# GpSimd's share of the k products in three instructions, with VectorE's share ordered ahead of them

## The chip, the cores and the metric

The kernel runs on one core of a Trainium2 chip. The metric is the time of one execution in microseconds (us) on the device, as a median of several runs. A profile of one execution gives the durations of the single instructions. Some runs are slow (over 1.5% above the fastest of the same kernel). Ratios and means below are of fast runs, unless slow ones are named; medians are of all runs.

## The reference

A linear attention with polynomial features feeds a feed-forward layer:

```python
# q, k, v: (4 batches, 4 heads, 1088, 32); S1, S2: (8, 32)
def phi(x):                       # 64 features: all products of 8 by 8 projections
    a = einsum('rd,bhsd->bhsr', S1, x); b = einsum('rd,bhsd->bhsr', S2, x)
    return einsum('bhsi,bhsj->bhsij', a, b).reshape(*x.shape[:-1], 64)
q_p, k_p = phi(q), phi(k)
kv = einsum('bhsf,bhsd->bhfd', k_p, v);  z = k_p.sum(axis=2)
attn = einsum('bhsf,bhfd->bhsd', q_p, kv) / (einsum('bhsf,bhf->bhs', q_p, z)[..., None] + 1e-6)
h = maximum(x @ w_in, 0)          # x: attn as 4352 tokens of 128; w_in: 128 x 2048
out = (h * h) @ w_out
```

## The kernel before

TensorE's time is filled by the feed-forward part: per step one matmul with w_in into PSUM (tile pg, L908), a Relu from PSUM to SBUF (gt, on ScalarE L918 or VectorE L920), a square (g, L902 or L929), and a matmul with w_out (po, L939). While one chunk of tokens goes through it, the attention of later chunks is slipped in between by a planner, which places each small task into a step of the loop. The tasks in question are the features of k of batch n = 1, 2, 3: TensorE makes the projections (qk from kq, L431), VectorE turns them (fs, L352), and the 64 products per token and head are made half on VectorE and half on GpSimd (kp, L361):

```python
    def a_kp2(b, g):                               # L357
        fs = st[b, "fs"]
        ...
        (nc.vector if g == 0 else nc.gpsimd).tensor_tensor(
            out=_ap(st[b, "kp2"], 0, 128, 128 * NT * g, [[64, 2 * NT], [8, 8], [1, 8]]),
            in0=_ap(fs, 0, 128, 2 * g, [[32, 2 * NT], [4, 8], [0, 8]]),
            in1=_ap(fs, 0, 128, 2 * g + 1, [[32, 2 * NT], [0, 8], [4, 8]]),
            op=mult,
        )
    ...
    def k_tasks(n):                                # L1288
        for g in range(2):
            P.add(("fs", n, g), "DVE", 0.45, [("kf", n)], a_fs, n, g, slow=n > 1 and 1.2)
        P.at["X"] = max(P.at["X"], P.at["fs", n, 1])
        P.add(("kp", n, 1), "POOL", 3.15, [("fs", n, 1)], a_kp2, n, 1)
        if n == 1:
            x_tasks(0, 2)
        P.add(("kp", n, 0), "DVE", 1.36, [("fs", n, 0)], a_kp2, n, 0, slow=n > 1 and 1.5)
```

`_ap(tile, partition, partitions, offset, [[step, count], ...])` is a free access pattern in fp32 elements. In batch 1 the chain de, rd, rb, x, ax (`x_tasks`) runs on VectorE and ScalarE between the two products. In batches 2 and 3 VectorE has another turn (qT, L325) just ahead of its product and a Relu of the feed-forward part (L920) just behind it.

Of the kernel before, what the change touches and what calls it, by code (L numbers as in the profile page):

```python
# [15 lines left out]
def _ap(t: bass.AP, p0: int, np_: int, off: int, free):  # L16

    p = list(t.ap)[0]
    return bass.AP(
        t.tensor, t.offset + p0 * p[0] + off, [[p[0], np_]] + [list(d) for d in free]  # L20
    )
# [52 lines left out]
def kernel(  # L74
# [22 lines left out]
    NT = (S + 127) // 128  # L97
# [141 lines left out]
    st = {}  # L239
# [114 lines left out]
                _ap(kf, 0, 128, 0, [[16, 2 * NT], [2, 8], [1, 2]]),  # L354
            )

    def a_kp2(b, g):  # L357
        fs = st[b, "fs"]
        if (b, "kp2") not in st:
            st[b, "kp2"] = wpool.tile([128, 2 * 128 * NT], F32, tag="kp2", name="kp2")  # L360
        (nc.vector if g == 0 else nc.gpsimd).tensor_tensor(  # L361
            out=_ap(st[b, "kp2"], 0, 128, 128 * NT * g, [[64, 2 * NT], [8, 8], [1, 8]]),
            in0=_ap(fs, 0, 128, 2 * g, [[32, 2 * NT], [4, 8], [0, 8]]),
            in1=_ap(fs, 0, 128, 2 * g + 1, [[32, 2 * NT], [0, 8], [4, 8]]),
            op=mult,
        )

# [737 lines left out]
    for lo, n in ((0, 2), (2, 3)):  # L1105
        nc.vector.tensor_tensor(
            out=_ap(kp4, 0, 128, 256 * lo, [[64, 4 * n], [8, 8], [1, 8]]),
            in0=_ap(fs4, 0, 128, 64 * lo, [[16, 4 * n], [2, 8], [0, 8]]),
            in1=_ap(fs4, 0, 128, 64 * lo + 1, [[16, 4 * n], [0, 8], [2, 8]]),
# [53 lines left out]
    P = _Plan(NS + 4, {"PE": 0.95, "DVE": 1.2, "ACT": 0.6, "POOL": 5.0, "SP": 9.0})  # L1163
    for m in range(B * 3 - 1):
        b, ch = divmod(m, 3)
# [98 lines left out]
    def x_tasks(b, ch):  # L1264
        if b == 0:
            P.add(("dT", b, ch), "DVE", 0.58, [("nd", b, ch)], a_dT, b, ch)
            P.add(("rd", b, ch), "DVE", 0.4, [("dT", b, ch)], a_rd, b, ch, lag=0)
            P.add(("rb", b, ch), "DVE", 0.58, [("rd", b, ch)], a_rb, b, ch, lag=0)
            P.add(("x", b, ch), "DVE", 0.56, [("rb", b, ch)], a_x, b, ch, lag=0)
        else:  # L1270
            P.at["x", b, ch] = P.at["nd", b, ch]
        P.add(("ax", b, ch), "ACT", 0.5, [("x", b, ch)], a_ax, b, ch)
        P.add(("sum", b, ch), "PE", 0.17, [("ax", b, ch)], a_sum, b, ch)
        P.add(("rs", b, ch), "DVE", 0.53, [("sum", b, ch)], a_rs, b, ch)
        if b > 0:
            P.add(("xs", b, ch), "DVE", 0.56, [("rs", b, ch)], a_xs, b, ch, lag=0)
        P.add(("s2", b, ch), "DVE", 0.53, [("sum", b, ch)], a_s2, b, ch)
        if b == 0:
            P.add(("xs", b, ch), "POOL", 0.95, [("rs", b, ch)], a_xs, b, ch)
            P.at["N"] = P.at["s2", b, ch]  # L1280
        else:
            P.at["N"] = max(P.at["s2", b, ch], P.at["xs", b, ch])
        P.add(("bt", b, ch), "POOL", 1.0, [("s2", b, ch)], a_beta, b, ch)
        if (b, ch) == (B - 1, 2):
            P.add(("bcol", b, ch), "DVE", 0.5, [("bt", b, ch)], a_bcol, b, ch, lag=3)
        ready(b, ch)

    def k_tasks(n):  # L1288
        for g in range(2):
            P.add(("fs", n, g), "DVE", 0.45, [("kf", n)], a_fs, n, g, slow=n > 1 and 1.2)  # L1290
        P.at["X"] = max(P.at["X"], P.at["fs", n, 1])
        P.add(("kp", n, 1), "POOL", 3.15, [("fs", n, 1)], a_kp2, n, 1)
        if n == 1:
            x_tasks(0, 2)
        P.add(("kp", n, 0), "DVE", 1.36, [("fs", n, 0)], a_kp2, n, 0, slow=n > 1 and 1.5)

    def turn_q(n, i):
        c0, c1 = 384 * i, min(384 * i + 384, S)
# [34 lines left out]
    P.add(("set", 1), "DVE", 0.6, [], a_set, 1, first=8)  # L1333
    nd_tasks(0, 2)
    k_tasks(1)
    kv_tasks(1)
    turn_q(1, 0)
# [4 lines left out]
    for m in range(3, 3 * B):  # L1342
        n, ch = divmod(m, 3)
        if m == 99:
            P.cap["DVE"] = CAP
        if ch == 0 and n + 1 < B:
            turn_k(n + 1)
        nd_tasks(n, ch)
        if True:
            x_tasks(n, ch)  # L1350
        if m + 1 < 3 * B:
            feature_tasks(*divmod(m + 1, 3))
        if False:
            x_tasks(n, ch)
        if ch == 0 and n + 1 < B:
            k_tasks(n + 1)
        if ch == 1 and n + 1 < B:
            kv_tasks(n + 1)
        if m + 2 < 3 * B:
            turn_q(*divmod(m + 2, 3))  # L1360
# [88 lines left out]
```

## Time and profile before

| | before |
|---|---|
| time, median of 3 runs (lowest, highest) | 200.17 us (199.97, 200.66) |
| span of the profiled run | 199.2 us |
| TensorE busy | 186.3 us, 94% |
| ScalarE, VectorE, GpSimd busy | 66%, 62%, 43% |
| product of 1152 elements on VectorE | 2.21, 4.34, 4.36 us |
| product of 1152 elements on GpSimd | 2.70 us, three times |

TensorE is full but for a few places, so the question at each place is which wait ends last in front of TensorE. The prediction shows the lines. Four instructions of TensorE serve below as marks along the run. They are from the timeline (start us, duration us, engine, line, operation); the first three are the k projections of batches 1, 2 and 3, the fourth is a projection of q behind batch 3's products:

```profile
29.70 0.69 PE L431 MATMUL qk<-kq,sk 64*32 64x288 f32 x16
...
57.01 0.72 PE L431 MATMUL qk<-kq,sk 64*32 64x288 f32 x16
...
101.17 0.71 PE L431 MATMUL qk<-kq,sk 64*32 64x288 f32 x16
...
116.54 0.56 PE L564 MATMUL qk<-qT,sw 64*64 64x160 f32 x8
```

In windows of 0.1 us the granted clock of this run is 0.50 from 113.3 to 116.7 us, behind batch 3's products, and 1.00 on both sides; these 3.4 us are called the half-speed window or the clock drop below.

The stretch from one mark to the next holds the products of one batch: 57.01 - 29.70 = 27.31 us for batch 1, 44.16 for batch 2, 15.37 for batch 3. Before the first mark lie 29.7 us of start, behind the last 82.7 us of tail.

### The profile page before, as it was taken

To read this page: it belongs to the slowest core of one execution; us is meant where nothing else is said; L and a number is where in the kernel's file an instruction comes from. 1 tells how busy PE (TensorE), PEld (TensorE's weight loads), DVE (VectorE), ACT (ScalarE), POOL (GpSimd) and SP (SyncE) were. 2 spreads that over 40 slices of the span, in tenths; PEclk is the share of its full clock that TensorE was granted. 3 is DMA by queue.
4 is the path that set the end of the run, shared out by engine and by line. 5 is a ranking of instruction groups with operands and counts; after the bars stand their busy time and mean duration, and the time that the engine had idled before them with its cause. 6 is when DMAs were issued, how large, how long until landed. Compare 5 with 4: busy or idle time off the path is not lost.

```text
span 199.2 us, 4283 instructions
## 1 busy us (share of the span) xinstructions
PE 186.3 (94%) x1468; PEld 108.4 (54%) x1468; DVE 123.5 (62%) x284; ACT 130.6 (66%) x322; POOL 85.0 (43%) x166
## 2 busy tenths in 40 slices
PE   7997999899999699999999599999999999999990
PEld 2663655365655346555656346555465655555980
DVE  3958868965649856374459745486291754637750
ACT  3335795767949566877759348569495766856840
POOL 5825545473329161534549123333646441351000
PEclk9999999999999999999999879999999999999999
DMA  5699243020256121422155120121022030200201
GB/s 171 173 303 276 71 106 142 0 43 0 53 112 181 40 33 35 129 41 51 27 121 160 33 31 19 34 41 38 21 42 60 0 63 21 33 10 0 43 0 33
DMA packets 30079, 13.91 MB, mean 70 GB/s; under 512 B 20202, under 2 KB 28778, under 8 KB 30058
## 3 DMA queue, kind: packets, MB, share of 16 engines
q1 hardware_dynamic: 29910, 13.58, 27.7%
q8 instruction: 11, 0.18, 0.4%
q14 instruction: 10, 0.08, 0.2%
q10 hardware_dynamic: 148, 0.07, 0.1%
HBM read 8.80 MB, written 2.23 MB: 55 GB/s over the span
## 4 chain that ended last, share of the span: by engine, by line
PE 77%; DVE 9%; issue 4%; DMA 3%; ACT 2%; SPq 2%; POOL 1%; ACTq 0%; DVEq 0%
PE po L939 48%; PE pg L908 13%; PE kvp L393 3%; PE ndn L637 2%; PE qk L564 2%; PE pt L956 2%; SPq L141 2%; PE nd L778 2%; DMA kn<-in_k_dram 1%; PE rep L1084 1%; DVE de L668 1%; ACT gt L918 1%; DMA ft<-ft 1%; DMA vn<-in_v_dram 1%; DVE fs L352 1%
## 5 line engine op out<-in xcount | busy, mean ns | idle before, releaser
L939 PE MATMUL po<-g,w_o 128*128 128x384 f32 (+3 forms) x386 | 145.1, 462 | 0.1
L918 ACT ACTIVATE gt<-pg 128x384 f32<-128x384 f32 (+2 forms) x139 | 65.2, 472 | 37.2 <-PE pg L908 36.5
L939 PEld LDWEIGHTS po<-g,w_o 128*128 128x128 f32 x386 | 65.9, 191 | 37.9 <-issue 20.1
L902 ACT ACTIVATE g<-gt 128x384 f32<-128x384 f32 (+1 forms) x146 | 72.2, 506 | 10.4 <-DVE gt L920 10.0
L908 PE MATMUL pg<-xT,w_in 128*128 128x384 f16 (+2 forms) x193 | 61.1, 318 | 4.7 <-DVE gt L920 4.1
L929 POOL TENSOR_TENSOR g<-gt 128x384 f32<-128x384 f32 (+1 forms) x44 | 34.4, 789 | 57.9 <-ACT gt L918 57.8
L920 DVE TENSOR_SCALAR gt<-pg 128x384 f32<-128x384 f32 (+1 forms) x54 | 28.8, 535 | 27.9 <-PE pg L908 20.3
L908 PEld LDWEIGHTS <-w_in 128*128 128x128 f16 x193 | 19.2, 99 | 22.9 <-issue 5.1
L599 POOL TENSOR_TENSOR qp<-tq,bs 128x384 f32<-128x384 f32 (+1 forms) x18 | 14.2, 810 | 16.9 <-DVE bs L591 16.9
L573 DVE STREAM_TRANSPOSE tq<-qk 128x384 f32<-128x384 f32 (+1 forms) x9 | 5.0, 561 | 13.7 <-PE qk L564 8.7
L738 POOL TENSOR_TENSOR bt<-s 128x384 f32<-128x384 f32 (+1 forms) x10 | 8.2, 816 | 7.2 <-DVE s L712 7.2
L361 DVE TENSOR_TENSOR kp<-fs 128x1152 f32<-128x1152 f32 x3 | 10.9, 3636 | 0.0
L985 DVE SCALAR_TENSOR_TENSOR sc<-po,bt 128x384 f32<-128x384 f32 (+1 forms) x9 | 4.8, 528 | 6.4 <-PE po L939 6.3
L361 POOL TENSOR_TENSOR kp<-fs 128x1152 f32<-128x1152 f32 x3 | 8.1, 2704 | 1.3 <-DVE fs L352 1.3
L971 POOL COPY br<-beta 32x3 f32<-32x3 f32 x32 | 5.8, 182 | 6.0 <-DVE beta L861 4.8
L720 DVE TENSOR_SCALAR rs<-ndn 128x384 uint32<-128x384 uint32 (+1 forms) x9 | 4.8, 536 | 3.7 <-PE ndn L704 3.5
L393 PEld LDWEIGHTS kvp<-kp,vn 128*32 128x32 f32 x288 | 5.4, 109 | 2.7 <-PE pg L908 1.6
L393 PE MATMUL kvp<-kp,vn 128*32 128x64 f32 x288 | 6.5, 223 | 0.0
L1060 PE MATMUL warm<-zero 128*128 128x512 f16 x16 | 5.2, 483 | 1.2 <-DVE zero L169 1.2
L325 DVE STREAM_TRANSPOSE qT<-qn 128x384 f32<-128x384 f32 (+1 forms) x12 | 6.3, 526 | 0.0
L956 PE MATMUL pt<-w_o,g 128*128 128x128 f32 x32 | 5.7, 274 | 0.0
L637 PE MATMUL ndn<-ft,kw 64*32 64x192 f32 (+1 forms) x144 | 5.6, 347 | 0.0
(147 smaller groups left out, 156.3 us busy)
## 6 DMA issues: line engine op xcount, KB each, us to landing
vn<-in_v_dram SPq DMA_DIRECT2D x32, 64.0 KB, 2.0
kn<-in_k_dram SPq DMA_DIRECT2D x3, 544.0 KB, 4.8
qn<-in_q_dram SPq DMA_DIRECT2D x3, 544.0 KB, 4.1
ft<-u SPq DMA_DIRECT2D x24, 48.0 KB, 1.9
out_dram<-oT SPq DMA_DIRECT2D x24, 48.0 KB, 1.9
w_in<-in_moe_w_in_dram SPq DMA_DIRECT2D x2, 512.0 KB, 8.4
w_o<-in_moe_w_out_dram SPq DMA_DIRECT2D x2, 512.0 KB, 9.9
ft<-ft SPq DMA_DIRECT2D x12, 48.0 KB, 1.8
```

What stands on the lines that cost most here:

```text
L361: (nc.vector if g == 0 else nc.gpsimd).tensor_tensor(out=_ap(st[b, "kp2"], 0, 128, 128 * NT * g, [[64, 2 * NT], [8, 8], [1, 8]]), in0=_ap( ...
L393: nc.tensor.matmul(st[b, "kvp"][32 * h : 32 * h + 32, 0:64], _ap(vn[b], 0, n, v0 + dv * h, [[1, 32]]), kp[0:n, at[h] : at[h] + 64], start= ...
L599: nc.gpsimd.tensor_tensor(out=_ap(qp, 0, 128, 0, [[32, m], [8, 4], [1, 8]]), in0=_ap(st[b, "tq", ch], 0, 128, 4 * e, [[32, m], [1, 4], [0, ...
L637: nc.tensor.matmul(nd[32 * h : 32 * h + 32, 512 * g : 512 * g + n], st[b, "kw"][64 * g : 64 * g + 64, 32 * h : 32 * h + 32], st[b, ch, "ft ...
L738: nc.gpsimd.tensor_tensor(out=bt[:, 0:n], in0=st[b, "s2", ch][:, 0:n], in1=st[b, "s2", ch][:, 0:n], op=mult)
L902: nc.scalar.activation(dst, src, Square)
L908: nc.tensor.matmul(pg[:, c0:c1], w_in[:, 128 * c : 128 * c + 128], st[b, "xT"][:, 384 * ch + c0 : 384 * ch + c1],)
L918: nc.scalar.activation(gt[:, c0:c1], pg[:, c0:c1], Relu)
L920: nc.vector.tensor_scalar(out=gt[:, c0:c1], in0=pg[:, c0:c1], scalar1=0.0, scalar2=None, op0=amax)
L929: (nc.vector if on[1] == "DVE" else nc.gpsimd).tensor_tensor(out=g2[:, c0:c1], in0=gt[:, c0:c1], in1=gt[:, c0:c1], op=mult)
L939: nc.tensor.matmul(st["po", b, ch][:, c0:c1], w_o[:, 128 * c : 128 * c + 128], g2s[i][1][:, c0:c1], start=first, stop=(c == NFF - 1), skip ...
L956: nc.tensor.matmul(st["pt"][:, 0:128], g2s[i][1][:, 0:128], w_o[:, 128 * c : 128 * c + 128], start=(c == 0), stop=(c == NFF - 1),)
```

## The change

The intent is that the two products of a batch no longer hold each other up: VectorE's comes first, right behind the turns, and GpSimd's follows in three pieces, so that a VectorE instruction that waits for GpSimd can start behind a piece and need not wait for the whole product. In the profile before, one did come in between two GpSimd instructions: xT ends at 39.52, VectorE's ob (from 38.77) at 39.92, and bt, which takes 1.04 us, at 40.50.

```diff
-    def a_kp2(b, g):
+    def a_kp2(b, g, lo=0, hi=NT):
         ...
-            out=_ap(st[b, "kp2"], 0, 128, 128 * NT * g, [[64, 2 * NT], [8, 8], [1, 8]]),
-            in0=_ap(fs, 0, 128, 2 * g, [[32, 2 * NT], [4, 8], [0, 8]]),
-            in1=_ap(fs, 0, 128, 2 * g + 1, [[32, 2 * NT], [0, 8], [4, 8]]),
+            out=_ap(st[b, "kp2"], 0, 128, 128 * (NT * g + lo), [[64, 2 * (hi - lo)], [8, 8], [1, 8]]),
+            in0=_ap(fs, 0, 128, 64 * lo + 2 * g, [[32, 2 * (hi - lo)], [4, 8], [0, 8]]),
+            in1=_ap(fs, 0, 128, 64 * lo + 2 * g + 1, [[32, 2 * (hi - lo)], [0, 8], [4, 8]]),
 ...
-        P.add(("kp", n, 1), "POOL", 3.15, [("fs", n, 1)], a_kp2, n, 1)
+        if n > 1:
+            P.add(("kp", n, 0), "DVE", 1.36, [("fs", n, 1)], a_kp2, n, 0, lag=0)
+        for i in range(3):
+            P.add(("kp", n, 1), "POOL", 0.95, [("kp", n, 0) if n > 1 else ("fs", n, 1)],
+                  a_kp2, n, 1, 3 * i, 3 * i + 3)
         if n == 1:
             x_tasks(0, 2)
-        P.add(("kp", n, 0), "DVE", 1.36, [("fs", n, 0)], a_kp2, n, 0, slow=n > 1 and 1.5)
+            P.add(("kp", n, 0), "DVE", 1.36, [("fs", n, 1)], a_kp2, n, 0)
```

## The prediction

> **What bounds the kernel now.** I read the page's busy table first: TensorE works 186.3 of 199.2 us, so an engine that is not TensorE matters only where it makes TensorE wait. The table of 40 slices (5 us each) tells where TensorE is not full: apart from start and end, the digits fall to 6 in slice 14 (64.7 to 69.7 us) and to 5 in slice 23 (109.6 to 114.5).
>
> ```profile
> PE 186.3 (94%) x1468; PEld 108.4 (54%) x1468; DVE 123.5 (62%) x284; ACT 130.6 (66%) x322; POOL 85.0 (43%) x166
> ...
> PE   7997999899999699999999599999999999999990
> ```
>
> Then the groups of line L361, the products of the k features, which the change touches. Each batch n = 1, 2, 3 has one such instruction on VectorE and one on GpSimd, of the same 1152 elements.
>
> ```profile
> L361 POOL TENSOR_TENSOR kp<-fs x3: 2699/2701/2711, 31.4 to 106.8; 128x1152 f32<-128x1152 f32 x3
> L361 DVE TENSOR_TENSOR kp<-fs x3: 2210/4342/4356, 35.4 to 107.2; 128x1152 f32<-128x1152 f32 x3
> ```
>
> The durations are minimum, median, maximum. GpSimd always takes 2.70 us; VectorE takes 2.21 us once and 4.34 and 4.36 us twice. The timeline tells why. These lines are batch 2 (start us, duration, engine, line):
>
> ```profile
> 62.60 2.70 POOL L361 TENSOR_TENSOR kp<-fs 128x1152 f32<-128x1152 f32 x1
> 62.61 0.47 DVE L325 STREAM_TRANSPOSE qT<-qn 128x320 f32<-128x320 f32 x1
> ...
> 63.00 4.34 DVE L361 TENSOR_TENSOR kp<-fs 128x1152 f32<-128x1152 f32 x1
> ...
> 67.27 0.54 DVE L920 TENSOR_SCALAR gt<-pg 128x384 f32<-128x384 f32 x1
> ...
> 67.86 0.32 PE L908 MATMUL pg<-xT,w_in 128*128 128x384 f16 x1 [1.81 <-DVE gt L920]
> ```
>
> GpSimd's product ends at 65.30, VectorE's at 67.34, which is 2.04 later and close to the 2.21 us of the undisturbed one: VectorE's instruction waited for the whole of GpSimd's. Behind it stands a Relu of the feed-forward part (gt, L920), and TensorE cannot refill that PSUM bank before: it idles until 67.86. The steps before are 0.81 us apart (L908 at 65.09), so 65.90 was due: 1.96 us lost. Batch 3 is the same at 106.76 to 112.04: L908 at 108.81, due at 109.62, came at 112.04, 2.42 us lost. Batch 1 differs, and there VectorE's product is not the victim:
>
> ```profile
> 31.43 2.70 POOL L361 TENSOR_TENSOR kp<-fs 128x1152 f32<-128x1152 f32 x1 [1.31 <-DVE fs L352]
> ...
> 31.78 2.38 DVE L668 TENSOR_SCALAR de<-dT 128x10 f32<-128x10 f32 x1
> ...
> 35.51 0.56 ACT L693 ACTIVATE ax<-x,tiny 128x320 bf16<-128x320 f32 x1 [1.43 <-DVE x L684]
> ```
>
> An addition on ten elements takes 2.38 us, ending at 34.16, right after GpSimd's 34.13. The chain de, rd, rb, x, ax hangs on it, and TensorE's small sum and the Relus and squares queued behind ax on ScalarE. TensorE's last matmul before is over at 35.34; with a sum between, the next L939 was due at about 35.66 and came at 36.91: 1.25 us lost. The three losses are 5.6 us.
>
> One cost comes behind the third. The windows view (last three numbers: clock, DMA share, GB/s) shows a slower TensorE clock only there:
>
> ```profile
> 108.00:112.00 4.00, 1.78 (x8) 0.88 (x6) 4.00 (x3) 1.69 (x4) 1.48 (x1) 1.00 0.27 66
> 112.00:116.00 4.00, 3.96 (x17) 1.83 (x24) 1.92 (x4) 1.84 (x4) 0.83 (x1) 0.66 0.24 35
> 116.00:120.00 4.00, 4.00 (x37) 2.15 (x22) 1.80 (x6) 2.53 (x6) 1.73 (x3) 0.91 0.06 10
> ```
>
> By 116.61, when the 16 ndn matmuls are done, it has cost some 1.2 us against batch 2's same steps (L908 to the end of ndn takes 3.07 us there, 67.86 to 70.93, and 4.57 here, 112.04 to 116.61; part of that is a wait for a Relu).
>
> [...] batch 2's transposes (ft, 61.66) and L728 (one PSUM, one SBUF input, 60.72) run at 0.57 and 0.56 us beside GpSimd products. [...] fs is read with a step of four fp32 elements here, at 2210/1152 = 1.9 ns per element, against 0.95/768 = 1.2 ns for batch 0's product (L1106), which reads with a step of two. So VectorE's own cost is 2.2 us, not the 1.36 that the source plans with. [...] A clock of 0.66 and 0.91 in the two stretches is what one half-speed window of 3.4 us makes (0.34 x 4 + 0.09 x 4 = 1.7 us of clock lost).
>
> **The change, part by part.** The order of the built instructions, compared engine by engine, shows less than the diff suggests. TensorE, ScalarE and SyncE are the same. On GpSimd the three products become three each of 384 elements, in the same place. On VectorE only batches 2 and 3 change: the product and the transpose qT swap places; in batch 1 the order stays. No wait is added between the two engines' products, so GpSimd does not wait for VectorE by a semaphore.
>
> (a) GpSimd pieces. 2.70/3 = 0.90 us each, near the 0.83 us of its other 384-element products; total unchanged. [...] GpSimd xT (to 39.52) and bt follow each other at once, VectorE's two-input ob (38.77) ends at 39.92, and bt takes 1.04 us where the 320-element products of L929 and L599 take 0.72 and 0.74 on average: ob came between.
>
> (b) Batch 1. de gets in after piece 1, at 31.43 + 0.90 = 32.33 instead of 34.13, 1.8 earlier. rd, rb, x take until 33.66 (35.48 before). ScalarE is free for ax at 34.08, ends at 34.6; then Relu to 35.0, square to 35.5, in time for the L939 due at 35.66. Gain 1.25 us. VectorE's product then waits for piece 3 (34.1) and ends at 36.2 instead of 37.61.
>
> (c) Batches 2 and 3. VectorE's product is ready at 62.61, where qT started; GpSimd's first piece at 62.60. It is nearly a tie, the same 10 ns in batch 3 (106.76 and 106.77). *GpSimd first:* VectorE runs from 63.5 to 65.6, qT adds 0.39, the Relu runs 65.95 to 66.5, L908 at 66.55: 1.3 gained of 1.96. Batch 3 likewise: product to 109.7, Relu 110.05 to 110.6, L908 at 110.65: 1.4 of 2.42. *VectorE first:* product to 64.8, Relu from 65.15, no stall in batch 2; in batch 3 L908 at 109.88, 2.15 gained. But batch 2 then meets the moves of ft by DMA: the last of the four is issued at 66.6 to 67.1 and needs 1.9 us to land, so at 69.05; TensorE's ndn, at 70.38 before, would be due at 68.42. Of 1.96 some 0.6 is lost, 1.35 stays.
>
> Sum: GpSimd first 1.25 + 1.3 + 1.4 = 3.95; VectorE first 1.25 + 1.35 + 2.15 = 4.75. The clock drop should vanish in both, since batch 3's pause shrinks from 2.25 us to 1 or less. But the run with this profile took 201.02 us and the timed ones 200.17, so I suppose that most timed runs do not have it, and count 0.2.
>
> GpSimd's later work does not suffer: its pieces end near 67.5 and 111.7; the next square comes at 69.72 and 113.83, each about 2 us earlier after the change, and k v (L393) is 10 us away.
>
> **The rivals.** *The pieces follow so closely that VectorE never gets between.* Then de still waits to 34.1, and in batches 2 and 3 the product with qT behind it ends 0.4 later: 200.2 to 201. Against it stands ob between xT and bt. *Something else takes the place of the wait.* TensorE runs earlier against DMA (the ft moves, above) and against ScalarE, which in 63 to 65 us is full (its squares release L939 with waits of 0.2 to 0.3 us per step); half the gain could go: 197.5 to 198. For it: ScalarE's 4.00 of 4.00 us busy in 60 to 64 us. Against it: it catches up as soon as Relus fall to VectorE, and I found its squares in time in (b) and (c). *The clock drop is in most of the timed runs:* then 1 us more is gained, 195.
>
> **Range and chances.** Tie weighted evenly: (3.95 + 4.75)/2 = 4.35, plus 0.2, less 0.35 because small waits usually return: 4.2 us, so 196.0. Low 194.7 is VectorE first with most of the clock gain; high 197.8 is half the gain. The 2% line is at 196.17, just beside the estimate, so faster gets only 0.54; slower would need the first rival and more.
>
> **What would show it.** Right: de under 1 us; VectorE's product in batches 2 and 3 at 3.1 us (GpSimd first) or 2.2 (VectorE first, GpSimd's first piece then near 3 us); the Relu behind it near 66 or 65; TensorE's slices 14 and 23 at 8 or 9; clock 1.00 throughout. Wrong: VectorE's product still at 4.3 us or more; or short, but TensorE waiting at ndn or on ScalarE squares for what was saved.

## The result, and the profile after

The changed kernel takes 194.74 us (median of 4 runs, 194.59 to 195.64) beside 200.41 us of the kernel before (4 runs, 199.97 to 201.84). The ratio is 0.971, with a 95% interval of 0.966 to 0.977, which is a gain of 4.6 to 6.9 us. Ratios here are the mean time of one kernel's fast runs over that of the other's of the same rounds, so they are not quite the ratio of the medians quoted. By the means (200.66 and 194.93) the gain is 5.7 us. I had predicted 4.2 us; the result is at or beyond the low end of my range, according to which of the two figures for before one starts from. So the direction was right and the size too small.

First the page's busy rows of the changed kernel, engines and the 40 slices, with the granted clock in tenths:

```profile
PE 184.9 (96%) x1468; PEld 108.2 (56%) x1468; DVE 118.6 (61%) x284; ACT 130.6 (68%) x322; POOL 91.0 (47%) x172
...
PE   7997999999999999999999999999999999999990
...
PEclk9999999999999999999999999999999999999999
```

The 6 and the 5 in TensorE's row are gone. VectorE is busy 4.9 us less, GpSimd 6.0 us more: the wait has moved from one engine to the other, and is counted as busy time on both. The groups of L361 (minimum, median, maximum in ns) show the same:

```profile
L361 POOL TENSOR_TENSOR kp<-fs x9: 1015/1032/3140, 31.5 to 107.8; 128x384 f32<-128x384 f32 x9
L361 DVE TENSOR_TENSOR kp<-fs x3: 2218/2232/2832, 33.7 to 103.7; 128x1152 f32<-128x1152 f32 x3
```

VectorE's product takes 2.2 us in batches 2 and 3; GpSimd's first piece takes up to 3.14 us there, which is its wait. The timeline of batch 2:

```profile
61.39 5.11 POOL L361 TENSOR_TENSOR kp<-fs 128x384 f32<-128x384 f32 x3
...
61.39 2.23 DVE L361 TENSOR_TENSOR kp<-fs 128x1152 f32<-128x1152 f32 x1
...
63.97 0.52 DVE L920 TENSOR_SCALAR gt<-pg 128x384 f32<-128x384 f32 x1
...
64.68 0.33 PE L908 MATMUL pg<-xT,w_in 128*128 128x384 f16 x1
```

Both products start in the same hundredth of a microsecond, VectorE's takes 2.23 us (2.21 where nothing held it up in the kernel before) while GpSimd's three pieces stretch to 5.11 us, and the Relu behind it comes at 63.97, in time: L908 carries no wait. Batch 1:

```profile
31.45 2.98 POOL L361 TENSOR_TENSOR kp<-fs 128x384 f32<-128x384 f32 x3 [1.31 <-DVE fs L352]
...
31.81 0.69 DVE L668 TENSOR_SCALAR de<-dT 128x10 f32<-128x10 f32 x1
...
34.01 0.55 ACT L693 ACTIVATE ax<-x,tiny 128x320 bf16<-128x320 f32 x1
```

The small addition de gets in behind the first piece and takes 0.69 us instead of 2.38; ax comes 1.5 us earlier. The windows around batch 3 (the last three figures of a line are the mean clock, the DMA share and GB/s) show no clock below 1.00:

```profile
104.00:108.00 4.00, 3.88 (x17) 2.22 (x16) 3.91 (x6) 3.61 (x9) 4.00 (x3) 1.00 0.45 136
108.00:112.00 4.00, 4.00 (x37) 1.85 (x36) 2.26 (x7) 2.16 (x5) 2.24 (x3) 1.00 0.30 45
```

And the four marks:

```profile
29.73 0.69 PE L431 MATMUL qk<-kq,sk 64*32 64x288 f32 x16
...
55.79 0.72 PE L431 MATMUL qk<-kq,sk 64*32 64x288 f32 x16
...
98.14 0.71 PE L431 MATMUL qk<-kq,sk 64*32 64x288 f32 x16
...
109.87 0.50 PE L564 MATMUL qk<-qT,sw 64*64 64x160 f32 x8
```

The stretches are 26.06, 42.35 and 11.73 us. So batch 1 gave 1.25 us, batch 2 1.81, batch 3 3.64; the tail grew by 0.3 us (82.7 to 83.0). Of batch 3's 3.64, the pause itself is 2.14: L908 lost 2.42 us before, and now it starts at 106.88 where 105.79 + 0.81 = 106.60 was due, 0.28 lost:

```profile
105.79 0.33 PE L908 MATMUL pg<-xT,w_in 128*128 128x384 f16 x1
...
106.88 0.32 PE L908 MATMUL pg<-xT,w_in 128*128 128x384 f16 x1
```

The other 1.50 us go with the half-speed clock behind the pause (0.50 from 113.3 to 116.7 us before, 1.00 in both windows here), a short wait for a Relu in it included; the run batch3_old below has the pause without the drop, and there this part is 15.37 - 13.84 = 1.53 us.

### The profile page after: what moved, and what is told of

It reads as the page before. It is cut to its first block, busy times and chain, and to the rows that moved or that the text cites.

```text
span 192.9 us, 4289 instructions
## 1 busy us (share of the span) xinstructions
PE 184.9 (96%) x1468; PEld 108.2 (56%) x1468; DVE 118.6 (61%) x284; ACT 130.6 (68%) x322; POOL 91.0 (47%) x172
## 3 DMA queue, kind: packets, MB, share of 16 engines
HBM read 8.80 MB, written 2.23 MB: 57 GB/s over the span
## 4 chain that ended last, share of the span: by engine, by line
PE 86%; DVE 4%; SPq 3%; DMA 2%; ACT 1%; issue 1%; POOL 1%; ACTq 0%
PE po L939 53%; PE pg L908 15%; PE kvp L393 3%; PE ndn L637 2%; PE warm L1060 2%; PE qk L564 2%; PE pt L956 2%; SPq L141 2%; PE nd L778 2%; PE rep L1084 1%; SPq L626 1%; DMA ft<-u 1%; ACT gt L918 1%; DVE kp L361 1%; DMA vn<-in_v_dram 1%
## 5 line engine op out<-in xcount | busy, mean ns | idle before, releaser
L939 PE MATMUL po<-g,w_o 128*128 128x384 f32 (+3 forms) x386 | 144.1, 459 | 0.0
L918 ACT ACTIVATE gt<-pg 128x384 f32<-128x384 f32 (+2 forms) x139 | 65.4, 473 | 36.3 <-PE pg L908 35.6
L939 PEld LDWEIGHTS po<-g,w_o 128*128 128x128 f32 x386 | 65.6, 190 | 33.3 <-ACT g L902 16.9
L908 PE MATMUL pg<-xT,w_in 128*128 128x384 f16 (+2 forms) x193 | 60.9, 317 | 0.7 <-ACT xT L880 0.3
L929 POOL TENSOR_TENSOR g<-gt 128x384 f32<-128x384 f32 (+1 forms) x44 | 34.9, 801 | 46.3 <-ACT gt L918 46.2
L908 PEld LDWEIGHTS <-w_in 128*128 128x128 f16 x193 | 19.1, 99 | 21.9 <-issue 4.1
L361 POOL TENSOR_TENSOR kp<-fs 128x384 f32<-128x384 f32 x9 | 13.2, 1498 | 1.3 <-DVE fs L352 1.3
L361 DVE TENSOR_TENSOR kp<-fs 128x1152 f32<-128x1152 f32 x3 | 7.3, 2427 | 0.0
```

What stands on the lines that cost most here:

```text
L361: (nc.vector if g == 0 else nc.gpsimd).tensor_tensor(out=_ap(st[b, "kp2"], 0, 128, 128 * (NT * g + lo), [[64, 2 * (hi - lo)], [8, 8], [1, ...
L908: nc.tensor.matmul(pg[:, c0:c1], w_in[:, 128 * c : 128 * c + 128], st[b, "xT"][:, 384 * ch + c0 : 384 * ch + c1],)
L918: nc.scalar.activation(gt[:, c0:c1], pg[:, c0:c1], Relu)
L929: (nc.vector if on[1] == "DVE" else nc.gpsimd).tensor_tensor(out=g2[:, c0:c1], in0=gt[:, c0:c1], in1=gt[:, c0:c1], op=mult)
L939: nc.tensor.matmul(st["po", b, ch][:, c0:c1], w_o[:, 128 * c : 128 * c + 128], g2s[i][1][:, c0:c1], start=first, stop=(c == NFF - 1), skip ...
```

## The experiments

The table gives the same stretches for each profiled run, from the same four marks, so that it can be read beside each experiment. The time up to the first mark is not touched by any edit, and yet it differs by up to 2.5 us between profiled runs; this is probably a large part of the noise in the timed medians (the timed runs have no profile to show it). The first four experiments ran on one chip, the last four on another, each beside its own runs of the kernel before (medians 202.13 and 200.64 us, means of the fast ones 201.58 and 200.77). So expected times, which start from 200.2 us, are to be compared by gains and ratios.

| kernel | to mark 1 | batch 1 | batch 2 | batch 3 | tail |
|---|---|---|---|---|---|
| before | 29.70 | 27.31 | 44.16 | 15.37 | 82.7 |
| changed | 29.73 | 26.06 | 42.35 | 11.73 | 83.0 |
| split_only | 32.15 | 26.06 | 42.59 | 12.26 | 82.4 |
| order_only | 31.45 | 27.31 | 42.44 | 11.73 | 83.0 |
| tie | 30.35 | 26.07 | 42.99 | 12.63 | 82.9 |
| de_reduce | 30.31 | 25.78 | 44.16 | 15.56 | 82.6 |
| after_again | 30.52 | 26.07 | 42.56 | 11.75 | 82.1 |
| batch3_old | 30.34 | 26.06 | 42.41 | 13.84 | 82.8 |
| layout | 30.57 | 25.86 | 42.40 | 11.45 | 82.7 |
| pieces63 | 30.33 | 26.48 | 42.55 | 11.73 | 82.3 |

**split_only: the pieces alone.** To the kernel before, with `a_kp2` taking lo and hi as in the change:

```diff
-        P.add(("kp", n, 1), "POOL", 3.15, [("fs", n, 1)], a_kp2, n, 1)
+        def three():
+            for i in range(3):
+                a_kp2(n, 1, 3 * i, 3 * i + 3)
+        P.add(("kp", n, 1), "POOL", 3.15, [("fs", n, 1)], three)
```

> The kernel before with GpSimd's products in three pieces and VectorE's order left as it was (qT ahead of the product). Theory [...]: batch 1 as in the changed kernel, de near 0.7 us and 1.2 us gained; in batches 2 and 3 GpSimd is first by 0.4 us, VectorE's product takes about 2.7 us instead of 4.34, the Relu behind it comes some 1.65 us earlier, 1.6 us gained in each. Sum 4.4 us, and 0.6 for the clock drop in the mean of the timed runs: about 195.5 us. Rival (the new order in VectorE does the work, the pieces add little): 199 us or more, VectorE's product still at 4 us.

Measured: correct; 196.94 us median (195.19 to 198.13, two of six runs slow), ratio 0.972 (0.966 to 0.977). The group of VectorE's products:

```profile
L361 DVE TENSOR_TENSOR kp<-fs x3: 2747/2765/2819, 36.2 to 106.8; 128x1152 f32<-128x1152 f32 x3
```

It takes 2.75 us where 2.7 was expected: it starts 0.4 us after GpSimd's first piece, waits for the rest of that piece, and the second piece waits for it. de took 0.70 us. The stretches shrink by 1.25, 1.57 and 3.11 us. The theory, that a VectorE instruction that GpSimd holds up starts at the first boundary between two GpSimd instructions, holds, and the rival falls: the pieces alone give nearly all of it. The median is 1.4 us higher than expected, but by the means of this chip the gain is 5.3 us, where 4.4 + 0.6 was expected; the profiled run came 2.4 us later to the first mark and its granted clock is 0.91 from 16 to 20 us and 0.67 from 20 to 24 already, ahead of anything that was changed.

**order_only: the order alone.** To the changed kernel (GpSimd's pieces 2 and 3 are replaced by an empty task, so that the plan stays the same):

```diff
-                  a_kp2, n, 1, 3 * i, 3 * i + 3)
+                  *((a_kp2, n, 1) if i == 0 else (int,)))
```

> The changed order on VectorE, GpSimd's products left whole (2.70 us). Theory: VectorE wins the tie in batches 2 and 3, as the changed kernel showed, so its product takes 2.2 us and GpSimd's 4.9; 1.8 and 2.1 us gained there as in the changed kernel; batch 1 keeps its 2.38 us of de and its loss of 1.2 us. Gain 3.9 and 0.6 for the clock: about 196. Rival (the pieces do the work): within 1 us of the kernel before, about 199.5.

Measured: correct; 197.59 us median (196.41 to 199.05), ratio 0.980 (0.976 to 0.985).

```profile
L361 POOL TENSOR_TENSOR kp<-fs x3: 2700/4811/4831, 33.2 to 106.8; 128x1152 f32<-128x1152 f32 x3
L361 DVE TENSOR_TENSOR kp<-fs x3: 2216/2217/2243, 37.1 to 106.8; 128x1152 f32<-128x1152 f32 x3
```

Batch 1 keeps its 27.31 us to the hundredth and its de of 2.38 us; batches 2 and 3 gain 1.72 and 3.64 us, with GpSimd's product stretched to 4.8 us because now it is the one that waits. Either half of the change repairs batches 2 and 3 almost alone; batch 1 is repaired by the pieces only. The median is 1.6 us above the expectation; by the means of this chip the gain is 3.9 us, where 4.5 was expected. Here too the profiled run was late at the first mark (31.45 us). Its mean clock is 0.984, and no stretch behind that mark is more than 0.1 us longer than in the profiles of before (batch 1) or changed (the others), so its drop lay ahead of the mark, as an estimate from these lengths.

**tie: who comes first.** To the changed kernel:

```diff
+    tie = cpool.tile([128, 64], F32)
...
+        if g == 0 and b > 1:
+            nc.vector.memset(tie[:], 0.0)
```

> The changed kernel with a small VectorE memset (64 columns, about 0.1 us) just ahead of the product in batches 2 and 3, so that GpSimd's first piece comes clearly first. Theory [...]: VectorE's product waits for one piece and takes about 3.0 us instead of 2.2; TensorE loses 0.6 us in batch 2 and 0.9 in batch 3 against the changed kernel: about 196.0 us, against 194.7. Rival (VectorE has priority whoever comes first): the product stays at 2.2 us, and the time within 0.3 us of the changed kernel.

Measured: correct; 196.51 us median (195.64 to 197.07), ratio 0.974 (0.970 to 0.978). Two lines of its timeline (the added lines shift L361 to L364) and batch 2's result:

```profile
62.02 5.02 POOL L364 TENSOR_TENSOR kp<-fs 128x384 f32<-128x384 f32 x3
...
62.10 3.08 DVE L364 TENSOR_TENSOR kp<-fs 128x1152 f32<-128x1152 f32 x1
...
66.09 0.32 PE L911 MATMUL pg<-xT,w_in 128*128 128x384 f16 x1 [0.62 <-DVE gt L923]
```

A start 0.08 us later costs VectorE a piece: 3.08 us instead of 2.23. So the theory, that the one that starts first holds up the other until it ends, fits here. Batch 2 takes 0.64 us more than in the changed kernel (0.6 expected), batch 3 0.90 more (0.9 expected). VectorE did not go first with GpSimd 0.08 us ahead; but it won a near tie, even where its start is recorded 0.01 us later (order_only, batch 2: GpSimd at 64.35 with 4.83 us, VectorE at 64.36 with 2.24).

**de_reduce: the addition in another form.** The theory is that a tensor_reduce does not wait for GpSimd's product where the tensor_scalar did (2.38 us). To the kernel before:

```diff
-        nc.vector.tensor_scalar(
-            out=de[:, 0:m], in0=_ap(st[b, "dT", ch], 0, 128, 0, [[32, m]]),
-            scalar1=1e-6, scalar2=None, op0=add,
+        nc.vector.tensor_reduce(
+            out=de[:, 0:m], in_=_ap(st[b, "dT", ch], 0, 128, 0, [[32, m], [1, 1]]), axis=AX, op=add,
         )
```

> The kernel before with batch 1's small addition de (tensor_scalar on ten elements) written as a tensor_reduce over one element, which drops the added 1e-6 (a result wrong by about that much, on purpose). Theory [...]: de takes about 0.2 us though GpSimd's whole product runs beside it; batch 1's loss of 1.2 us goes, batches 2 and 3 stay: about 199.0 against 200.2, ratio 0.994. Rival (a GpSimd product of this length holds up any VectorE instruction that follows): de still 2.3 us, time as before.

Measured: within the tolerance; 200.50 us median (200.02 to 201.32), ratio 0.9945 (0.991 to 0.998), as expected; the reading is the trace's.

```profile
32.39 0.17 DVE L668 TENSOR_REDUCE de<-dT 128x10 f32<-128x10 f32 x1
```

With GpSimd's product of 2.70 us running beside it from 32.0, it takes 0.17 us. So it is not GpSimd's length as such that held up the addition for 2.38 us, but the form of VectorE's instruction; why the form matters was not shown. Batch 1 gains 1.53 us, more than with the pieces; the others stay.

**after_again: a control** on the second chip, the changed kernel unaltered.

> The changed kernel unaltered, as a control on the chip of the next three. From batch 2's feature matmuls (qk<-kq) to the last qk<-qT of batch 3 the trace should again take 42.35 + 11.73 us, and no half-speed clock window should fall between 25 and 185 us. Ratio to the kernel before near 0.971.

Measured: correct; 195.84 us median (194.86 to 196.20, 7 runs), ratio 0.975 (0.972 to 0.979). By the means the gain is 5.1 us here and was 5.7 in the first comparison, so the last half microsecond of the gain is not certain. Batches 1 and 3 repeat within 0.02 us; batch 2 took 42.56 us instead of 42.35, so differences of 0.2 us there mean nothing. Its profiled run has a mean clock of 0.995, and no stretch behind the first mark is more than 0.21 us longer than in the first profile, so none has room for the 1.5 us of a clock drop. One of its seven runs has a mean clock of 0.988, the others 0.995 to 1.000.

**batch3_old: the clock drop.** To the changed kernel:

```diff
-        if n > 1:
+        if n == 2:
             P.add(("kp", n, 0), "DVE", 1.36, [("fs", n, 1)], a_kp2, n, 0, lag=0)
+        if n == 3:
+            P.add(("kp", n, 1), "POOL", 3.15, [("fs", n, 1)], a_kp2, n, 1)
+        else: ...the three pieces...
 ...
+        if n == 3:
+            P.add(("kp", n, 0), "DVE", 1.36, [("fs", n, 0)], a_kp2, n, 0, slow=1.5)
```

> The changed kernel with only batch 3's products as before (qT first, GpSimd's product whole). Theory: the pause of TensorE in batch 3 is back, 2.1 us more than in the changed kernel; and [...] the half-speed window of 3.4 us follows and costs another 1.5 us, which should be so in about half of the runs (mean clock 0.99 or less), as in 6 of 11 runs of the kernel before. Mean 2.1 to 3.6 us above the changed kernel, and the trace of batch 3 either 13.9 or 15.4 us. Rival (the clock drops belong to the chip or to the start, not to this pause): clock as in the changed kernel in all runs, 2.1 us above.

Measured: correct; 198.65 us median (197.23 to 199.18), ratio 0.988. The profiled run is one without a drop (mean clock 0.996) and takes 13.84 us in batch 3, 2.1 more than the control:

```profile
109.65 0.32 PE L908 MATMUL pg<-xT,w_in 128*128 128x384 f16 x1 [2.22 <-DVE gt L920]
```

Four of the six runs have a mean clock of 0.986 to 0.988 and take 198.6 to 199.2 us; the two with 0.996 and 0.998 take 197.2 and 198.0. The rival that the drops belong to the chip or the start alone falls. In which place of the unprofiled runs the drop lay is not seen; the profiles of before and de_reduce have it behind batch 3's pause (before: 0.50 from 113.3 us, 1.3 us after L908 had come at 112.04; de_reduce: 0.97 from 108 to 112 us and 0.61 from 112 to 116). Counted over all runs: of 34 runs of kernels with batch 3's pause (22 of before, slow ones included, and those of de_reduce and batch3_old) 19 have a mean clock of 0.990 or less; of 41 runs of kernels without it (the changed kernel, split_only, order_only, tie, after_again, layout, pieces63) 3 have, and two of these are the profiled runs of split_only (clock 0.67 from 20 to 24 us) and order_only (mean 0.984), whose drops lay ahead of the first mark. With fast runs alone it is 15 of 30 against 3 of 39. Why the drop follows the pause in one run and not in another, no run here shows.

**layout: the step of the reads.** To the changed kernel:

```diff
-                _ap(st[b, "fs"], 0, 128, 2 * g, [[32, 2 * NT], [4, 8], [1, 2]]),
+                _ap(st[b, "fs"], 0, 128, g, [[16, 2 * NT], [2, 8], [32 * NT, 2]]),
 ...
-            in0=_ap(fs, 0, 128, 64 * lo + 2 * g, [[32, 2 * (hi - lo)], [4, 8], [0, 8]]),
-            in1=_ap(fs, 0, 128, 64 * lo + 2 * g + 1, [[32, 2 * (hi - lo)], [0, 8], [4, 8]]),
+            in0=_ap(fs, 0, 128, 32 * lo + g, [[16, 2 * (hi - lo)], [2, 8], [0, 8]]),
+            in1=_ap(fs, 0, 128, 32 * (NT + lo) + g, [[16, 2 * (hi - lo)], [0, 8], [2, 8]]),
 ...  # and the gram matmul reads each plane with step 1 instead of 2
```

> The changed kernel with the k features stored in two planes, so that both products read fs with a step of two fp32 elements instead of four; the same arithmetic. Theory [...]: VectorE's product falls from 2.2 to about 1.4 us (1.2 ns per element, as batch 0's), GpSimd's pieces from 1.02 to about 0.83. TensorE waits for it only 0.3 us in batch 3 by now, so the time falls by 0.3 us at most. Rival (the 2.2 us come from the two inputs or the length): the product stays at 2.2.

Measured: correct; 195.00 us median (194.72 to 196.68), ratio 0.972 (0.968 to 0.976).

```profile
L361 POOL TENSOR_TENSOR kp<-fs x9: 875/881/2071, 32.7 to 107.6; 128x384 f32<-128x384 f32 x9
L361 DVE TENSOR_TENSOR kp<-fs x3: 1318/1320/1628, 34.8 to 104.7; 128x1152 f32<-128x1152 f32 x3
```

The product falls to 1.32 us, GpSimd's pieces from 1.03 to 0.88; the turns fs that write the planes rise from 0.46 to 0.68 us. So the step of the reads set the cost of this product: 2.22 us with a step of four fp32 elements, 1.32 with a step of two. Why the step matters was not shown. Batch 3's stretch falls by 0.30 us, as expected, batch 1's by 0.2. This kernel's mean of 195.23 us beside the control's 195.70 is the best, but the intervals of the two overlap, so it is faster than the kernel before and not shown to be faster than the changed one.

**pieces63: where the first boundary lies.** To the changed kernel, batch 1 only:

```diff
-                  a_kp2, n, 1, 3 * i, 3 * i + 3)
+                  *(((a_kp2, n, 1, 0, 6), (int,), (a_kp2, n, 1, 6, 9))[i] if n == 1 else (a_kp2, n, 1, 3 * i, 3 * i + 3)))
```

> The changed kernel with batch 1's GpSimd product in two pieces, 768 and 384 elements, instead of three of 384. Theory (VectorE gets in at the first boundary): de ends at the end of the first piece, so it takes about 1.5 us instead of 0.69; ax comes 0.8 us later, ScalarE's square after it misses the L939 due, and 0.5 to 0.8 us of batch 1's 1.25 us are lost again; batches 2 and 3 unchanged. Time 0.6 us above the changed kernel. Rival (the number of pieces or their start costs matter, not where the first ends): no slower.

Measured: correct; 195.78 us median (195.18 to 197.61), ratio 0.976 (0.972 to 0.981).

```profile
32.41 1.55 DVE L668 TENSOR_SCALAR de<-dT 128x10 f32<-128x10 f32 x1
```

de takes 1.55 us, as the length of the first piece demands, and batch 1 loses 0.41 us against the control, a little less than the 0.5 to 0.8 expected. The mean time rises by 0.3 us (196.03 against 195.70), too little to be told from noise. With one piece, a first piece of 768 and one of 384, de takes 2.38, 1.55 and 0.69 us.

## Why the prediction was right and wrong

The account of the waits was right. What failed is the sizing of four terms of the sum, each too low: the even weighting of the tie (by 0.4 us), the term for the moves of ft (0.45), the count for the clock (some 0.2) and the deduction for small waits (0.35).

*What bounds the kernel, and the wait.* This held at every step. The wait behind a GpSimd instruction went as the prediction has it: another form of the same addition did not wait (0.17 us in de_reduce instead of 2.38); a boundary let VectorE in (its product at 2.75 us in split_only instead of 4.34, de at 1.55 in pieces63); the product that came first held up the other (tie: VectorE's at 3.08 us instead of 2.23; order_only: GpSimd's at 4.81 and 4.83 instead of 2.70). By what mechanism the two engines hold each other up was not shown. The three losses of 1.25, 1.96 and 2.42 us that I read from the trace became gains of 1.25, 1.81 and 2.14. That the first agrees to the hundredth is in part luck: the matmul L939 behind the sum came 1.43 us earlier after the mark, and some 0.2 us were lost again a little later (below).

*"Tie weighted evenly."* This step failed. VectorE won in both batches of every profile in which the two start within 0.01 us (changed kernel, order_only, after_again, layout, pieces63), and in batch 2 of batch3_old: its product took 2.22 to 2.25 us there, 1.32 in layout. The trace before had GpSimd's start 0.01 us ahead of VectorE's next instruction, and from that alone I could not tell. The even weighting took 0.4 us off the case that came. Its other branch was sized well: in tie, where GpSimd comes first, batch 2 gains 1.17 us and batch 3, without the 1.50 of the clock, 1.24, where the prediction has 1.3 and 1.4.

*"The last of the four is issued at 66.6 to 67.1 and needs 1.9 us to land, so at 69.05 [...] some 0.6 is lost."* The term was mis-sized. The 1.9 us count from the start of the issue, not from its end. In the view of tile ft of the changed kernel (batch 2):

```profile
L626 SPq DMA_DIRECT2D ft<-u x4: 508/516/591, 62.3 to 65.4; - x4
...
DMA to landing us min/median/max: 1.9/1.9/1.9
```

The last issue starts at 65.4, so it lands at 67.3, and the ndn matmuls that need it began at 67.20:

```profile
67.20 0.71 PE L637 MATMUL ndn<-ft,kw 64*32 64x192 f32 x16
```

They took 0.71 us instead of 0.56: 0.15 us were lost, not 0.6. With this and VectorE first, the sum of the pauses is 1.25 + 1.81 + 2.14 = 5.2 us, where the record has 4.75 for this branch and 4.35 for the average.

*"I suppose that most timed runs do not have it, and count 0.2."* This was too low, by an amount that stays uncertain. It rested on the difference between one profiled run (201.02 us) and three timed ones. Of 18 later fast runs of the kernel before, 6 had a mean clock of 0.990 or less, and these took 202.0 us on average against 200.8 for the others: as an estimate from these, 6/18 x 1.2 = 0.4 us of the mean was due to drops. The four slow ones all had 0.978 or 0.979; with them counted the estimate is 0.8 us, but a difference that slow runs make is not used here. Some of the lowest may have a drop at the start as well.

*"Less 0.35 because small waits usually return."* This is not confirmed as a term of its own. Small waits did return, but inside the stretches, where they are counted already: 0.15 us at ndn in batch 2, and one in batch 1 of the same kind as the old one, in the other direction. There VectorE's product now runs while a square on GpSimd (L929) is due, which takes 1.46 us instead of 0.99, and the L939 that needs it waits 0.58 us instead of 0.23. The tail grew by 0.3 us in this profile, but the same kernel in after_again has a tail of 82.1 us, shorter than before, so the tail shows nothing.

The sum in place of mine is 5.2 + 0.4 = 5.6 us. The measured gain is 5.7 us by the means, 5.1 in the control, with an interval of 4.6 to 6.9, so the close agreement proves little; the gains of the stretches are the firmer part. Piece (a) was a little too cheap: the three pieces of batch 1 take 2.98 us together instead of 2.70, some 0.14 us per cut, with no visible effect on the time. The rivals did not come: VectorE gets between the pieces (de at 0.69 us), and neither ScalarE nor DMA took the place of the wait, but for the 0.15 us at ndn.

## What to carry to other kernels

Where a short VectorE instruction stands in a chain that the bound engine waits for, look at its duration in the trace rather than at its size; if it is several times too long and ends with a GpSimd instruction (here de with 2.38 us), cut the GpSimd instruction (de then took 0.69 us) or change the form of the VectorE one (0.17 us) before moving anything to another engine. For the wait of de the first boundary is what counted (2.38, 1.55 and 0.69 us behind a first piece of 1152, 768 and 384 elements), so a short first piece and a long rest may do as well; this was not run. When a pause of TensorE is removed, count what the pause brought with it too, here a half-speed clock that went with a single pause of 2.2 us in about half of the runs (15 of 30 fast runs with the pause had a mean clock of 0.990 or less, 3 of 39 without it), and judge that from the mean clock of many runs and not from one.
